# Two windowed attentions on one core: new schedule tables, and layer A's value matmuls two head groups at a time

## The chip, the cores and the metric

The kernel runs on one core of a Trainium2 chip. The metric is the device time of one execution in microseconds (us). Three runs of the kernel before took 1783.95, 1785.1 and 1788.92 us, median 1785.1. One more execution was profiled.

The core's engines run side by side, each through its own instructions in program order: TensorE (PE: matmuls, and weight loads as PEld), VectorE (DVE), ScalarE (ACT), GpSimd (POOL) and SyncE (SP, which here issues copies). They wait for each other on semaphores only.

## The reference

Two attention layers over separate inputs of 2048 rows and 1024 columns, 32 heads of 32, all in float32; their outputs are joined along the last axis.

```python
qkv = (x @ wqkv) ...; q, k, v = qkv[0], qkv[1], qkv[2]; scale = Dh ** -0.5
# layer A: 8 keys per query, every second position back
W, dil = 8, 2
logits = einsum("bhsd,bhswd->bhsw", q, kg) * scale      # kg, vg: gathered keys, values
o_A = softmax(where(mask, logits, -1e9)) @ vg ; out_A = o_A @ wo
# layer B: the 256 keys up to the query
scores = einsum("bhqd,bhkd->bhqk", q, k) * scale
mask = (i - j >= 0) & (i - j < 256)
o_B = softmax(where(mask, scores, -1e9)) @ v ; out_B = o_B @ wo
return concatenate([out_A, out_B], -1)
```

## The kernel before

**Units.** The work is eight units in order: units 0 to 3 are layer B's four stretches of 512 rows ("dense"), units 4 to 7 layer A's ("window"). Layer A's rows are sorted into even and odd ones first, so that a step of two positions becomes a step of one. In each unit the 32 heads are eight groups of four, numbered s = 0 to 7.

**Exact products.** A float32 operand is split into a rounded high part and the rest, and each product is three matmuls (`TERMS`). Splitting a weight or an x tile that was loaded into `raw` takes a cast (L232 on ACT or L235 on DVE) and a subtraction on DVE (L238). Loads into `raw` go out on POOL's queue (L181), three buffers in turn; a buffer's next load goes out when the split of the tile in it is done.

**Work on PE, per unit.** Projections of q and k: per group two blocks of 24 matmuls of 128x128 by 512 (L614). Values: one part of four groups and two of two groups (L683). The output projection of the unit before: eight blocks of 24 (L747). These form one long list, `gemm`, whose order the tables `V_AT`, `O_AT`, `EDGES_V` write out: which slot s holds which value part and output block, and at which item of a unit's last slot the next unit's x tiles ("x0" to "x3") and first weights ("q0", "v0", "v1", "k7") are split.

**Attention of a dense group.** Scores in 16 matmuls (L1024), each into one of four score banks (ring `rs`); row maximum on DVE (L1029), exponential and row sum on ACT (L1034). Then the logarithm of the sums, a small matmul that turns it over (L1063), scores again the other way round (L1108), exponential into `pbuf` (L1115), masks on POOL or DVE (L1093, L1096), and the values in 64x32 tiles of the array (L1173).

**Attention of a window group.** `window(u, s)`: 64 score matmuls in 32x64 tiles (L820) into the four banks of `rs`; mask, softmax on DVE and ACT (L828 to L856) in `band[s % 2]`; two transposes (L859) and sixteen copies on ACT (L868, L871) into `wide[s % 2]`; then `values`, 64 or 72 matmuls in 64x32 tiles (L892) into two banks, the single bank of ring `ro` and one of `rs`; last `overlap` adds the halves where windows overlap and splits the result into an `ot` tile (L981 to L994), an operand of the output projection. `ot` tiles and x tiles share 19 seats (`seats_x`). The scores of group s+2 wait until the values of group s have been issued (`done["o"]`), since they share `band` and `wide`, and until all four score banks are free.

**Who sets the order.** Everything is issued by hand-made order: a planner runs at build time. `Clock` keeps an estimate of when each engine is free; four lists (`aux`, `twos`, `ones`, `gemm`) hold PE's items in order, each with a `ready` time, and the loop at the end always takes the item that could start first. `ones` holds the scores, `twos` the later steps of attention. Only the order comes out of it; on the chip the semaphores decide. The tables shift its estimates: `PACE` per unit (offsets for masks, keys, row data and values, bias of splits, and last the step k of a block at which the next weight is split), `LATE` (added to the time at which a group's q and k are ready for scores), `HOLD` (added to the time at which its values may start), `AHEAD` (added to the step k). `seats_x.used`, `give` and `defer` keep account of what comes free.

Of the kernel before, what the change touches and what calls it, by code (L numbers as in the profile page):

```python
# [36 lines left out]
O_AT = ({2: (0, 1), 3: (2, 3), 4: (4, 5), 5: (6, 7)}, {3: (0, 1), 4: (2, 3), 5: (4, 5), 7: (6, 7)}, {2: (0, 1), 3: (2, 3), 4: (4, 5), 5: (6, 7)}, {2: (0, 1), 3: (2, 3), 4: (4, 5), 6: (6, 7)}, {3: (0, 1), 4: (2, 3), 5: (4, 5), 6: (6, 7)}, {2: (0, 1), 3: (2, 3), 4: (4, 5), 5: (6, 7)}, {1: (0,), 2: (1,), 3: (2, 3), 4: (4,), 5: (5,), 6: (6, 7)}, {1: (0,), 2: (1, 2), 3: (3, 4), 5: (5, 6), 6: (7,)})
EDGE_AT = (0, 1, 2, 3, 4, 5, 6, 7)
EDGES_V = (((2, 'k7'), (5, 'v0'), (14, 'q0'), (15, 'x0'), (18, 'v1'), (27, 'x1'), (29, 'x2'), (33, 'x3')), ((1, 'k7'), (1, 'x0'), (10, 'v0'), (11, 'v1'), (20, 'x1'), (20, 'x2'), (32, 'q0'), (33, 'x3')), ((3, 'k7'), (10, 'v0'), (13, 'v1'), (15, 'x0'), (22, 'x1'), (26, 'x2'), (27, 'q0'), (31, 'x3')), ((5, 'k7'), (6, 'v0'), (12, 'x0'), (14, 'q0'), (17, 'v1'), (18, 'x1'), (24, 'x2'), (32, 'x3')), ((2, 'k7'), (5, 'x0'), (10, 'v0'), (16, 'v1'), (17, 'x1'), (22, 'x2'), (26, 'q0'), (28, 'x3')), ((0, 'k7'), (7, 'v0'), (13, 'x0'), (14, 'v1'), (17, 'q0'), (20, 'x1'), (26, 'x2'), (31, 'x3')), ((2, 'k7'), (10, 'x0'), (10, 'v0'), (15, 'v1'), (16, 'x1'), (26, 'x2'), (29, 'q0'), (33, 'x3')), ((2, 'k7'), (7, 'v0'), (14, 'x0'), (17, 'v1'), (17, 'q0'), (21, 'x1'), (25, 'x2'), (29, 'x3')))
EDGES_K = (((0, 'x0'), (2, 'x1'), (5, 'q0'), (6, 'x2'), (10, 'x3'), (15, 'k0')), ((1, 'q0'), (1, 'x0'), (3, 'x1'), (7, 'x2'), (11, 'x3'), (16, 'k0')), ((0, 'x0'), (4, 'x1'), (4, 'q0'), (8, 'x2'), (12, 'x3'), (16, 'k0')), ((0, 'x0'), (2, 'x1'), (5, 'q0'), (6, 'x2'), (10, 'x3'), (15, 'k0')), ((1, 'q0'), (1, 'x0'), (3, 'x1'), (7, 'x2'), (11, 'x3'), (16, 'k0')), ((0, 'x0'), (2, 'x1'), (5, 'q0'), (6, 'x2'), (10, 'x3'), (15, 'k0')), ((0, 'x0'), (4, 'x1'), (4, 'q0'), (8, 'x2'), (12, 'x3'), (16, 'k0')), ((0, 'x0'), (2, 'x1'), (5, 'q0'), (6, 'x2'), (10, 'x3'), (15, 'k0')))  # L40
LATE = ((7, 0, 1.5, 0, 0, 0, 0, 0), (1.5, 3, 5.5, 2, 0, 0, 0, 0), (0, 1.5, 0, 0, 0.5, 3, 0, 0), (0, 0, 0, 0, 0, 0, 0, 0), (0, 0, 0, 4, 0, 0, 0, 0), (0, 0, 0, 0, 0, 0, 0, 0), (0, 0, 0, 0, 0, 0, 0, 0), (0, 0, 0, 0, 0, 0, 0, 0))
ROWS = ((0, 0, 0, 0, 0, 0, 0, 0), (0, 0, 0, 0, 0, 0, 0, 0), (0, 0, 0, 0, 0, 0, 0, 0), (0, 0, 0.4, 0, 0, 0, 0, 0), (0, 0, 0, 0, 0.2, 0, 0, 0), (0, 0, 0, 0, 0, 0, 0, 0), (0, 0, 0, 0, 0, 0, 0, 0), (0, 0, 0, 0, 0, 0, 0, 0))
HOLD = ((0, 1.2, 0, 0, 0, 0, 0, 0), (0, 0, 0, 0, 0, 0, 0, 0), (0.6, 0, 0, 0, 0, 0, 0, 0), (0, 0, 0, 0, 0, 0, 0, 1.2), (0, 0, 0, 0, 0, 0, 0, 0), (0, 0, 0, 0, 0, 0, 0, 0), (-0.4, 0, 0, 0, 0, 0, 0, 0), (0, 0, 0, 0, 0, 0, 0, 0))
AHEAD = ((0, 0, 0, 2, 0, 0, 0, 0), (0, 0, 0, 0, 0, 0, 0, 0), (1, 0, 0, 3, 0, 0, 0, 0), (0, 0, 0, 0, 3, 0, 3, 0), (0, 0, 0, 0, 0, 2, 0, 0), (0, 0, 0, 0, 0, 0, 0, 0), (2, 0, 0, 0, 0, 0, 0, 0), (0, 0, 0, 0, 0, 0, 0, 0))
EARLY, WARM = 1.0, 10
ONES_AT = 5.0, 34.0
TERMS = ((0, 0), (0, 1), (1, 0))
# [2 lines left out]
class Clock:  # L50
# [6 lines left out]
    HOLD = dict(sp=0.63, act=0.35, pool=0.6)  # L57
# [202 lines left out]
def kernel(ctx, tc, xs, wqk, wv, wo, outs, units):  # L260
# [67 lines left out]
    for p in plan:  # L328
# [19 lines left out]
        else:  # L348
            u = p[1] - 1
# [15 lines left out]
    seats_x = Tiles(xpool, ck)  # L365
# [113 lines left out]
    rg, rs, ro, rx = Ring(psg, 2, "g"), Ring(pss, NS, "s"), Ring(pso, 1, "o"), Ring(psx, 1, "x")  # L479
# [7 lines left out]
    def latest(*ts):  # L487
        return None if any(t is None for t in ts) else max(ts)


    def qk_items(u, s):
# [54 lines left out]
        def evac(t, ps, bank):  # L546
# [7 lines left out]
            def low():  # L554
# [86 lines left out]
    def v_items(u, part):  # L641
# [149 lines left out]
    def window(u, s):  # L791


        has_halo = units[u][3]
        buf = s % 2
        hg = u * NG + s
        vp, vc = vparts[parts_of(u)][s]
        v = vbufs[parts_of(u)][vp]
# [4 lines left out]
        def p16():  # L803
            return band[buf][:, :1536].rearrange("p (i c) -> p i c", c=96)[:, :, 24:]

        h = {}

        def scores_ready():
            return latest(rs.empty(), done["stack"].get((u, s)),
# [64 lines left out]
                h["p"] = t + PACE[u][3] + HOLD[u][s]  # L874

        def values_ready():
            if not seats_x.free:
                return None
            return latest(done["v"].get((u, vp)), h.get("p"), ro.when(), rs.when())

        def values():
            h["o"], _ = ro.take()
            h["o2"], bank = rs.take()
            halves = [h["o"], h["o2"]]
            blocks = [(-1, 1, 0, 8)] if has_halo else []
            blocks += [(b, i, P * b + 64 * i, min(72, S - P * b - 64 * i)) for b in range(4) for i in range(2)]
            seen = set()
            for b, i, q0, w in blocks:
                c = 136 * b + 8 + 64 * i if b >= 0 else 0
                r = slice(64 * i, 64 * i + 64)  # L890
                for j in range(4):
                    nc.tensor.matmul(halves[i][32 * j:32 * j + 32, q0:q0 + w],  # L892
                                     v[r, (4 * u + b) % 6, vc + 32 * j:vc + 32 * j + 32], wide[buf][r, j, c:c + w],
                                     start=(i, j) not in seen, stop=True, skip_group_check=True)
# [440 lines left out]
```

## Time and profile before

| | |
|---|---|
| median of three runs | 1785.1 us |
| profiled execution | 1786.24 us |
| its span, first to last instruction | 1784.5 us |
| granted PE clock, mean | 0.999 |
| DVE, ACT, POOL busy | 71%, 59%, 20% |
| HBM read, written | 164.63 MB, 23.07 MB |

How to read the rows: the page gives busy time per engine; PE's is modelled from pipelined matmuls, so that starts, not durations, tell what a matmul costs in a run of them. In the timeline a row has its start, its length, engine, line, operation, output<-inputs, tile of the array, shape and count of merged instructions; square brackets hold the idle time of the engine before it and what ended that.

### The profile page before, as it was taken

The numbers are of one execution on the slowest core, as the hardware profiler recorded it, in microseconds if no ns is written. First come the engines' busy times: TensorE is split into PE (matmuls) and PEld (weight loads), VectorE is DVE, ScalarE is ACT, GpSimd is POOL, SyncE is SP. The second block draws the span as 40 slices with busy tenths as digits, with TensorE's granted clock in tenths as the row PEclk, the third lists the DMA queues.
The fourth block names the chain that finished last, engine by engine and source line by source line (L and its number), as shares of the span: only waits on it lengthen the run. The fifth ranks groups of instructions, "written<-read, shape, count | busy, mean of one in ns | idle before, by whom it ended". The sixth has DMA issues, their size and how long they took to land.

```text
span 1784.5 us, 39512 instructions
## 1 busy us (share of the span) xinstructions
PE 1770.5 (99%) x15210; PEld 1472.7 (83%) x15210; DVE 1268.0 (71%) x2742; ACT 1054.9 (59%) x2630; POOL 365.3 (20%) x776
## 2 busy tenths in 40 slices
PE   9999999999999999999999999999999999999999
PEld 7788888888888888888888888878888888888887
DVE  5668777777777779766667486876678666857863
ACT  5677666765667666676667355554555354534552
POOL 3222322123222313222233300110001100110000
PEclk9999999999999999999999999999999999999999
DMA  6556654647455456454653344444434443543432
GB/s 207 154 154 166 174 146 145 166 134 213 129 152 165 145 156 179 136 158 119 173 159 122 126 130 131 145 132 129 139 123 136 143 136 114 156 139 128 130 104 83
DMA packets 109724, 257.52 MB, mean 144 GB/s; under 512 B 14560, under 2 KB 29920, under 8 KB 109536
## 3 DMA queue, kind: packets, MB, share of 16 engines
q0 software_dynamic: 41760, 152.06, 27.6%
q1 hardware_dynamic: 58560, 86.15, 18.1%
q10 hardware_dynamic: 9216, 16.78, 2.5%
q8 instruction: 120, 1.97, 0.4%
q14 instruction: 68, 0.56, 0.1%
HBM read 164.63 MB, written 23.07 MB: 105 GB/s over the span
## 4 chain that ended last, share of the span: by engine, by line
PE 90%; DVE 4%; ACT 3%; DMA 2%; issue 1%; POOL 0%; SPq 0%; POOLq 0%; DVEq 0%; ACTq 0%
PE g L614 31%; PE g L747 16%; PE g L683 13%; PE s L1108 6%; PE x L614 6%; PE s L1024 5%; PE o L1173 3%; PE x L747 3%; PE x L683 2%; PE s L820 1%; DVE w L238 1%; PE x L1173 1%; DMA raw<-wv 1%; PE s L892 1%; ACT wide L868 1%
## 5 line engine op out<-in xcount | busy, mean ns | idle before, releaser
L614 PE MATMUL g<-x,w 128*128 128x512 f32 x2568 | 643.1, 393 | 0.8 <-ACT x L232 0.5
L614 PEld LDWEIGHTS g<-x,w 128*128 128x128 f32 x2568 | 476.4, 189 | 90.1 <-ACT x L232 1.0
L238 DVE TENSOR_TENSOR w<-raw,w 128x512 fp32r<-128x512 f32 x514 | 336.1, 695 | 44.6 <-ACT w L232 38.1
L1029 DVE CUSTOM_DVE_ANT_0 s<-s,mask_d 128x384 f32<-128x384 f32 (+2 forms) x512 | 262.1, 554 | 100.7 <-PE s L1024 99.6
L683 PE MATMUL g<-w,x 128*128 128x256 f32 (+1 forms) x1872 | 329.6, 320 | 1.2 <-DVE w L238 0.6
L1034 ACT ACTIVATE s<-s,nm 128x384 f32<-128x384 f32 (+2 forms) x512 | 273.8, 536 | 67.3 <-DVE nm L1029 65.7
L683 PEld LDWEIGHTS g<-w,x 128*128 128x128 f32 x1872 | 276.1, 190 | 25.0 <-DVE w L238 1.7
L747 PE MATMUL g<-ot,w 128*128 128x512 f32 x1200 | 296.2, 393 | 0.0
L747 PEld LDWEIGHTS g<-ot,w 128*128 128x128 f32 x1200 | 221.8, 188 | 43.4
L1093 POOL TENSOR_SCALAR_AFFINE_SELECT pbuf<-pbuf 128x256 f32<-128x256 f32 (+1 forms) x445 | 182.6, 435 | 212.8 <-ACT pbuf L1115 202.3
L1115 ACT ACTIVATE pbuf<-s 128x512 f32<-128x512 f32 (+1 forms) x368 | 188.9, 602 | 56.3 <-PE s L1108 50.8
L235 DVE CAST w<-raw 128x1024 fp32r<-128x1024 f32 x181 | 125.9, 695 | 67.9 <-PE g L614 24.6
L181 POOL DMA_DIRECT2D raw<-wqk x126 | 68.0, 540 | 511.9 <-DVE w L238 317.7
L1024 PE MATMUL s<-kst,qst 96*128 96x384 f32 (+2 forms) x512 | 142.2, 339 | 2.8 <-ACT s L1034 2.6
L868 ACT COPY wide<-wide 32x256 f32<-32x256 f32 x256 | 103.4, 404 | 45.8 <-DVE wide L859 42.2
L1108 PE MATMUL s<-qst,kst 128*128 128x128 f32 (+2 forms) x704 | 126.4, 307 | 0.6 <-ACT pbuf L1115 0.3
L614 PE MATMUL x<-x,w 128*128 128x512 f32 x504 | 121.8, 393 | 0.0
L1108 PEld LDWEIGHTS s<-qst,kst 128*128 128x128 f32 x704 | 107.9, 189 | 16.9 <-ACT s L1034 2.3
L1024 PEld LDWEIGHTS s<-kst,qst 96*128 96x128 f32 x512 | 92.7, 189 | 24.1 <-ACT s L1034 6.6
L614 PEld LDWEIGHTS x<-x,w 128*128 128x128 f32 x504 | 93.3, 188 | 20.2
L1034 ACT ACTIVATION_READ_ACCUMULATOR s<-s,nm 128x1 f32 x512 | 105.5, 206 | 0.2
L181 POOL DMA_DIRECT2D raw<-wv x72 | 46.4, 644 | 257.8 <-DVE w L238 97.1
(111 smaller groups left out, 1930.6 us busy)
## 6 DMA issues: line engine op xcount, KB each, us to landing
raw<-wqk POOLq DMA_DIRECT2D x126, 512.0 KB, 4.0
raw<-wv POOLq DMA_DIRECT2D x72, 512.0 KB, 4.4
raw<-wo POOLq DMA_DIRECT2D x64, 512.0 KB, 3.9
qst<-nat SPq DMA_DIRECT2D x96, 256.0 KB, 4.1
kst<-nat SPq DMA_DIRECT2D x96, 256.0 KB, 5.4
raw<-xs POOLq DMA_DIRECT2D x28, 512.0 KB, 4.9
outs<-ost ACTq DMA_DIRECT2D x56, 256.0 KB, 2.6
kst<-halo SPq DMA_DIRECT2D x72, 128.0 KB, 2.8
```

Of the source, the lines that this page charges most:

```text
L235: nc.vector.tensor_copy(t[:, 0, :], raw)
L238: nc.vector.tensor_tensor(t[:, 1, c:c + 512], raw[:, c:c + 512], t[:, 0, c:c + 512].bitcast(F32), op=ALU.subtract)
L614: nc.tensor.matmul(h["ps"], h["w"][:, a, k * P:(k + 1) * P], xt[u][k][:, b, :], start=(k == 0 and i == 0), stop=(k == NK - 1 and i == 2))
L683: nc.tensor.matmul(ps, xt[u][kw * g + k][:, a, p0:p0 + P], h["w"][g][:, c, k], start=(first and t == 0 and half == 0), stop=(last and t == 2),
L747: nc.tensor.matmul(h["ps"], w[:, a, c:c + P], ot[u, k][:, b, :], start=(k == 0 and i == 0), stop=(k == NK - 1 and i == 2))
L868: nc.scalar.copy(diag[r:r + 32, :, :, c:c + 32], pieces[r:r + 32, :, :, 1 + i % 2, :])
L1024: nc.tensor.matmul(ps[:, :n], q[0:96, j, b * P:(b + 1) * P], kk[0:96, j, c0:c1], start=True, stop=True)
L1029: nc.vector.tensor_tensor_reduce(ps[:, :n], ps[:, :n], mask[:, cut:full], scale=-1.0, scalar=BIG, op0=ALU.add, op1=ALU.min, accum_out=nm)
L1034: nc.scalar.activation(ps[:, :n], ps[:, :n], AF.Exp, bias=nm, scale=-1.0, accum_out=sm)
L1093: nc.gpsimd.affine_select(w, w, pattern=[[0, m], [step, n]], compare_op=ALU.is_ge, fill=0.0, base=base, channel_multiplier=chan)
L1108: nc.tensor.matmul(ps[:, x:x + w], kk[:, j, 256 + kb * P:256 + (kb + 1) * P], q[:, j, q0:q0 + w], start=True, stop=True)
L1115: nc.scalar.activation(w, ps[:, :m * n].rearrange("p (j n) -> p j n", j=m), AF.Exp)
```

## The change

First, the values of a window group can be issued together with its neighbour's. `PAIRS` names the pairs, by unit: groups 0 and 1 and groups 4 and 5 of unit 4, 0 to 3 in two pairs of unit 5, 0 and 1 of unit 6, 0 and 1 and 4 and 5 of unit 7. The even group of a pair adds no item to `twos`; the odd group's item runs both groups' values in a row, and then both `overlap`s. It becomes ready when both groups' softmaxes are done, two seats are free and all four score banks are. The even group's first bank is then one of `rs` instead of `ro`'s.

```diff
+PAIRS = ((), (), (), (), (0, 2), (0, 1), (0,), (0, 2))
...
-        h = {}
+        h = pairs[hg % 2] = {}
...
         def values_ready():
-            if not seats_x.free:
+            if len(seats_x.free) < len(both):
                 return None
-            return latest(done["v"].get((u, vp)), h.get("p"), ro.when(), rs.when())
+            return latest(done["v"].get((u, vp)), *[x.get("p") for x in both], ro.when(),
+                          rs.when() if alone else rs.empty())
 
         def values():
-            h["o"], _ = ro.take()
+            own = ro if alone or s % 2 else rs
+            h["o"], first_bank = own.take()
             h["o2"], bank = rs.take()
...
+            return lambda: overlap(u, s, h, bank, own, first_bank, 0 if has_halo else 1)
+
+        alone = s // 2 not in PAIRS[u]
+        h["values"], both = values, [h] if alone else list(pairs)
+
+        def two():
+            ends = [x["values"]() for x in both]
+
             def after():
-                overlap(u, s, h, bank, 0 if has_halo else 1)
+                for f in ends:
+                    f()
 
             return after
 
-        return [Item(scores_ready, scores, CW)], [Item(values_ready, values, C3 + CP)]
+        return [Item(scores_ready, scores, CW)], [Item(values_ready, two, C3 + len(both) * CP)] if alone or s % 2 else []
...
-            ro.give(0, e)
+            own.give(first_bank, e)
```

Second, entries of the tables. In each line stand unit and place, old and new value:

```text
PACE     unit 1 mask bias for POOL 0.1 -> 0.4; unit 2 last entry 0 -> 2; unit 3 value cost 0.0 -> 0.4, last 2 -> 1;
         unit 4 last 2 -> 3; unit 7 bias of splits 0.5 -> -0.5
O_AT     unit 2: blocks 6, 7 in slot 6, were in 5
         unit 3: {2: (0,), 3: (1, 2, 3), 4: (4, 5), 5: (6,), 7: (7,)}, was {2: (0, 1), 3: (2, 3), 4: (4, 5), 6: (6, 7)}
EDGES_V  unit 1: q0 at 28, was 32;  unit 2: x1 at 19, was 22, x2 at 30, was 26;  unit 3: x2 at 28, was 24
         unit 5: x0, x1, x2, x3 at 11, 18, 24, 29, were 13, 20, 26, 31
         unit 6: x0 at 8, was 10; v0 at 11, was 10
LATE     unit 0 group 3: 0 -> 1.5
         unit 1 groups 4 to 7: 0, 0, 0, 0 -> -0.5, 0.5, 4, 4.5
         unit 2 groups 0, 3, 6, 7: 0, 0, 0, 0 -> 3, 4, -0.5, 4;  unit 3 group 0: 0 -> 2
HOLD     unit 1 group 4: 0 -> 1.2;  unit 2 groups 2, 7: 0, 0 -> 1.6, -0.4;  unit 3 group 0: 0 -> 1.2
AHEAD    unit 1 group 4: 0 -> -2;  unit 2 group 7: 0 -> 1;  unit 3 group 6: 3 -> 4
```

More of the change, by code (lines that the diff above doesn't have):

```diff
@@ L34 @@
 ORDER = (0, 1, 2, 3, 4, 5, 6, 7)
-PACE = ((0.4, 2.4, 0.1, 0.1, 0.4, -99, 4), (0.1, 1.8, 0.3, 0.1, 0.4, -99, 2), (0.1, 0.6, 0.3, 0.1, 0.0, -99, 0), (0.2, 2.4, 0.3, 0.1, 0.0, -99, 2), (6.0, 8.0, 0.5, 0.5, 1, 2), (2.0, 6.0, 1.5, 0.2, 1, 2), (4.0, 7.0, 0.5, 0.2, 1, 3), (4.0, 7.0, 0.5, 0.0, 1, 1))
+PACE = ((0.4, 2.4, 0.1, 0.1, 0.4, -99, 4), (0.4, 1.8, 0.3, 0.1, 0.4, -99, 2), (0.1, 0.6, 0.3, 0.1, 0.0, -99, 2), (0.2, 2.4, 0.3, 0.1, 0.4, -99, 1), (6.0, 8.0, 0.5, 0.5, 1, 3), (2.0, 6.0, 1.5, 0.2, 1, 2), (4.0, 7.0, 0.5, 0.2, 1, 3), (4.0, 7.0, -0.5, 0.0, 1, 1))
@@ L36 @@
 V_AT = ({0: 0, 4: 1, 7: 2}, {0: 0, 3: 1, 7: 2}, {0: 0, 5: 1, 7: 2}, {0: 0, 5: 1, 7: 2}, {0: 0, 4: 1, 7: 2}, {0: 0, 6: 1, 7: 2}, {0: 0, 6: 1, 7: 2}, {0: 0, 6: 1, 7: 2})
[L37 removed]
+O_AT = ({2: (0, 1), 3: (2, 3), 4: (4, 5), 5: (6, 7)}, {3: (0, 1), 4: (2, 3), 5: (4, 5), 7: (6, 7)}, {2: (0, 1), 3: (2, 3), 4: (4, 5), 6: (6, 7)}, {2: (0,), 3: (1, 2, 3), 4: (4, 5), 5: (6,), 7: (7,)}, {3: (0, 1), 4: (2, 3), 5: (4, 5), 6: (6, 7)}, {2: (0, 1), 3: (2, 3), 4: (4, 5), 5: (6, 7)}, {1: (0,), 2: (1,), 3: (2, 3), 4: (4,), 5: (5,), 6: (6, 7)}, {1: (0,), 2: (1, 2), 3: (3, 4), 5: (5, 6), 6: (7,)})
@@ L42 @@
 ROWS = ((0, 0, 0, 0, 0, 0, 0, 0), (0, 0, 0, 0, 0, 0, 0, 0), (0, 0, 0, 0, 0, 0, 0, 0), (0, 0, 0.4, 0, 0, 0, 0, 0), (0, 0, 0, 0, 0.2, 0, 0, 0), (0, 0, 0, 0, 0, 0, 0, 0), (0, 0, 0, 0, 0, 0, 0, 0), (0, 0, 0, 0, 0, 0, 0, 0))
-HOLD = ((0, 1.2, 0, 0, 0, 0, 0, 0), (0, 0, 0, 0, 0, 0, 0, 0), (0.6, 0, 0, 0, 0, 0, 0, 0), (0, 0, 0, 0, 0, 0, 0, 1.2), (0, 0, 0, 0, 0, 0, 0, 0), (0, 0, 0, 0, 0, 0, 0, 0), (-0.4, 0, 0, 0, 0, 0, 0, 0), (0, 0, 0, 0, 0, 0, 0, 0))
-AHEAD = ((0, 0, 0, 2, 0, 0, 0, 0), (0, 0, 0, 0, 0, 0, 0, 0), (1, 0, 0, 3, 0, 0, 0, 0), (0, 0, 0, 0, 3, 0, 3, 0), (0, 0, 0, 0, 0, 2, 0, 0), (0, 0, 0, 0, 0, 0, 0, 0), (2, 0, 0, 0, 0, 0, 0, 0), (0, 0, 0, 0, 0, 0, 0, 0))
+HOLD = ((0, 1.2, 0, 0, 0, 0, 0, 0), (0, 0, 0, 0, 1.2, 0, 0, 0), (0.6, 0, 1.6, 0, 0, 0, 0, -0.4), (1.2, 0, 0, 0, 0, 0, 0, 1.2), (0, 0, 0, 0, 0, 0, 0, 0), (0, 0, 0, 0, 0, 0, 0, 0), (-0.4, 0, 0, 0, 0, 0, 0, 0), (0, 0, 0, 0, 0, 0, 0, 0))
@@ L45 @@
+AHEAD = ((0, 0, 0, 2, 0, 0, 0, 0), (0, 0, 0, 0, -2, 0, 0, 0), (1, 0, 0, 3, 0, 0, 0, 1), (0, 0, 0, 0, 3, 0, 4, 0), (0, 0, 0, 0, 0, 2, 0, 0), (0, 0, 0, 0, 0, 0, 0, 0), (2, 0, 0, 0, 0, 0, 0, 0), (0, 0, 0, 0, 0, 0, 0, 0))
+PAIRS = ((), (), (), (), (0, 2), (0, 1), (0,), (0, 2))
 EARLY, WARM = 1.0, 10
@@ L444 @@
     halo = [[dram.tile([P, 2, 256], F32, name=f"halo{i}_{s}") for s in range(NG)] for i in range(2)]
+    pairs = [None, None]
     xt, xready, ot, rows = {}, {}, {}, {}
@@ L967, in join, with overlap @@
         ck.defer(r, add)
-    def overlap(u, s, h, bank, first):
+    def overlap(u, s, h, bank, own, first_bank, first):
         hg = u * NG + s
```

4 lines of the change are left out of this document (2 added, 2 removed).

## The prediction

> **What bounds the kernel now.** I read the page first, then the busy time by stage, then what TensorE (PE) waited for, and last the instructions in order of time around the waits and around two visits to small tiles.
>
> ```profile
> span 1784.5 us, 39512 instructions
> PE 1770.5 (99%) x15210; PEld 1472.7 (83%) x15210; DVE 1268.0 (71%) x2742; ACT 1054.9 (59%) x2630; POOL 365.3 (20%) x776
> PE 90%; DVE 4%; ACT 3%; DMA 2%; issue 1%; POOL 0%; SPq 0%; POOLq 0%; DVEq 0%; ACTq 0%
> ```
>
> The chain of work that ended last is PE for 90%, so only three things can move the end: PE instructions that go or come, the time PE loses when it changes between whole-array and small-tile matmuls, and the time in which it waits. The next view gives the busy time in six stretches: layer B's unit 0 and the start of unit 1, the rest of unit 1, unit 2, unit 3, then layer A in two halves.
>
> ```profile
> 0.00:326.00 326.00, 321.27 (x2233) 264.80 (x2234) 227.89 (x627) 222.70 (x597) 94.10 (x235) 1.00 0.60 165
> 326.00:488.00 162.00, 159.72 (x1219) 132.96 (x1218) 122.99 (x317) 105.52 (x273) 42.01 (x83) 0.99 0.56 159
> 488.00:742.00 254.00, 253.41 (x2020) 213.16 (x2019) 194.00 (x511) 173.53 (x446) 67.77 (x137) 1.00 0.54 155
> 742.00:1017.00 275.00, 275.00 (x2112) 230.39 (x2112) 181.52 (x465) 179.35 (x452) 86.00 (x188) 1.00 0.49 142
> 1017.00:1383.00 366.00, 364.39 (x3806) 302.32 (x3805) 271.53 (x412) 192.76 (x443) 38.27 (x68) 1.00 0.43 135
> ```
>
> After a width and PE's busy time stand PEld, DVE, ACT and POOL; near the end is the granted clock. Unit 1 is the one that sticks out: 2.28 us of open idling in 162 us and the only clock below 1.00; unit 3 idles not at all. Who made PE wait, in total, times, longest:
>
> ```profile
> PE s L1024 <- ACT s L1034: 2.6, 4, 0.9
> PE x L683 <- DVE w L238: 1.1, 1, 1.1
> PE s L1063 <- DVE hl L1055: 0.7, 2, 0.6
> PE g L683 <- DVE w L238: 0.6, 1, 0.6
> PE g L683 <- ACT vbuf L633: 0.5, 1, 0.5
> ```
>
> So all the waiting there is to win is a handful of single events. A steady run of whole-array matmuls gives the unit of account:
>
> ```profile
> 1498.61 4.24 PE L614 MATMUL g<-x,w 128*128 128x512 f32 x18
> 1502.69 0.52 PE L683 MATMUL x<-w,x 128*128 128x256 f32 x3
> ```
>
> Eighteen starts in 1502.69 - 1498.61 = 4.08 us: 0.227 us each (the 4.24 us includes the last one's pipelined tail).
>
> **The change, part by part. (a) Seven pairs.** A visit of one group of heads to the 64x32 tiles looks like this:
>
> ```profile
> 1042.71 2.20 PE L747 MATMUL g<-ot,w 128*128 128x512 f32 x9
> 1044.85 0.27 PE L892 MATMUL o<-wide,vbuf 64*32 64x72 f32 x4
> ...
> 1045.45 0.27 PE L892 MATMUL s<-wide,vbuf 64*32 64x64 f32 x4
> 1045.65 1.66 PE L747 MATMUL g<-ot,w 128*128 128x512 f32 x6
> 1047.14 1.07 PE L747 MATMUL x<-ot,w 128*128 128x512 f32 x4
> ```
>
> From 1042.71 to 1047.14 are 4.43 us, for 15 whole-array matmuls (15 x 0.227 = 3.40) and one visit: 1.03 us. Inside, 60 of its 64 matmuls start within 0.60 us, so all 64 take 0.64 to 0.66. The rest, 0.37 to 0.39 us, is the price of going in and out: on entry 2.14 us for nine where 2.04 is due (0.10), some 0.14 between the last tile and the next whole matmul, and 0.13 more in the six behind it (1.49 us for 6 x 0.227 = 1.36). A pair keeps both groups' 128 matmuls and drops one such price. At most 0.39 is saved; at least the entry's 0.10, if the loss behind a visit grows with its length. No visit of 128 matmuls is in the trace; I take 0.35, close to the one measured. 7 x 0.35 = **-2.4 us** (bounds -0.7 and -2.7).
>
> What it moves: the even group's values wait for the odd group's softmax, and the pair needs all four score banks free where one was needed. Behind it stand only the scores of the next two groups. In unit 5 group 1's values and group 2's scores are:
>
> ```profile
> 1229.11 0.21 PE L892 MATMUL s<-wide,vbuf 64*32 64x8 f32 x4
> ...
> 1235.61 0.94 PE L820 MATMUL s<-pbuf 32*64 32x72 f32 x64
> ```
>
> Group 2's scores already come 6.5 us after group 1's values, so with groups 0 and 1 together at 1229 they need not move, and projections fill PE meanwhile. I cost the delay at 0; without this cover it would be one late split per pair (a rival below). Each pair's ACT and DVE instructions stay the same in number, back to back; no DMA is added.
>
> **(b) The last part of unit 1.** Here are PE's and DVE's instructions where the next unit begins; then two stretches with the granted clock third from the end (0.89, 0.53); then two pieces of the chain of work:
>
> ```profile
> 437.80 0.51 PE L1024 MATMUL s<-kst,qst 96*128 96x384 f32 x2
> 439.21 0.44 PE L1024 MATMUL s<-kst,qst 96*128 96x384 f32 x1 [0.90 <-ACT s L1034]
> 440.29 0.69 PE L1024 MATMUL s<-kst,qst 96*128 96x384 f32 x1 [0.64 <-ACT s L1034]
> 440.78 5.41 PE L614 MATMUL g<-x,w 128*128 128x512 f32 x17
> ...
> 437.77 0.69 DVE L235 CAST w<-raw 128x1024 fp32r<-128x1024 f32 x1
> 438.49 1.29 DVE L238 TENSOR_TENSOR w<-raw,w 128x512 fp32r<-128x512 f32 x2
> ...
> 441.83 0.56 DVE L1029 CUSTOM_DVE_ANT_0 s<-s,mask_d 128x384 f32<-128x384 f32 x1
> ...
> 437.90:440.98 3.08, 1.54 (x6) 0.97 (x5) 3.01 (x7) 2.24 (x6) 0.72 (x1) 0.89 0.96 250
> 440.98:443.90 2.92, 2.92 (x9) 2.25 (x8) 2.88 (x8) 1.24 (x4) 0.73 (x1) 0.53 0.83 229
> 425.44 0.71 PE g L683 x6
> 426.68 0.18 PE s L1024
> ```
>
> Four score matmuls, 0.18 us each when nothing holds them (the last row), take 2.98 us until the next projection: 2.26 lost. DVE does no score's maximum from 437.77 to 441.83, because the split of unit 2's first weights ("q0") and of two x tiles stands in its queue. Then the clock falls to 0.53, and the 17 projections start over 5.41 - 0.39 = 5.02 us (0.39 is one matmul's tail, from the steady run: 4.24 - 17 x 0.2267) where 16 x 0.227 = 3.63 are due: 1.39 more. Together 3.65 us, over half of it hidden from the list of waits.
>
> The Trainium skill, "TensorE: Matmul & The Clock Gate", section "Why this matters for your kernels", asks only that PE has no idle gap over about 3 us. By that rule this stall would cost no clock, (b) would be worth at most 2.26 and the sum 1.4 us less; the trace has the fall after 1.54 us of idling spread over 3.08, so the measurement decides.
>
> The new tables move q0's split four list items ahead (32 to 28; an item of six half-width matmuls takes 0.71 us, the last row but one), so 2.8 us, its load through POOL's queue with it, and hold back the scores of groups 6 and 7 of unit 1 by up to 4 and 4.5 us in the planner's account. The split's 1.98 us leaves this spot. I take **-3.3** (bounds 0, if another collision takes its place, and -3.65).
>
> **(c) The rest of layer B's tables.** They touch group 3 of unit 0, and units 1 to 3: hold-backs, look-ahead positions, five output blocks one slot away, more masks offered to POOL. No instruction is added; the order of all that follows changes. At stake are the other two score waits (2.6 - 1.5 = 1.1) and the log-sum's 0.7. New small waits will come; I take **-0.5** (bounds -1.8, and +3.65 for one new stall like (b)'s). An output block in another slot is the same 24 matmuls: 0.
>
> **(d) Layer A's edges.** x tiles of units 6 and 7 are split two items earlier or one value block one later. They answer to the two DVE waits of 1.1 and 0.6 and, through unit 4's look-ahead moved from step 2 to 3, to the 0.5. An earlier split needs an earlier load through POOL's queue; PE has no wait for a DMA in the list, so that has cover. In unit 7 the splits lean by 1 us more towards DVE, where no wait for a split is on the list: 0. I take **-0.7** (bounds -2.2 and, mirrored, +2.2).
>
> Sum: -2.4 - 3.3 - 0.5 - 0.7 = -6.9. The profiled execution took 1786.24 us (span 1784.5 and 1.7 around it), so 1779.3 for a like one; it lies 1.1 above the median of 1785.1, and for the median I say **1778.2 us**.
>
> **The rivals.** *Pairs pay, the tables do not.* Unit 1's stall turns up elsewhere and small waits trade places: only (a), 1785.1 - 2.4 = 1782.7. For it: (b) is one accident of two queues, and any new order can make another. Against: unit 3 shows 275 us without one.
>
> *Slower: the new order makes more such stalls.* Place: score matmuls of units 1 to 3 meeting weight splits on DVE; price 3.65 each with the clock. If (b)'s stays and three more come, +11.0 - 2.4 = +8.6: 1793.7. From the first extra one (+1.3) the kernel is slower than before, and past two (+4.9) measurably so. For it: ten groups are held back or let go by new amounts at once. Against: one in four units now.
>
> *The pair chokes the queues.* Two softmaxes side by side hold up a weight split at each pair, at the 1.1 us of the longest wait for a split: 7 x 1.1 - 2.4 = +5.3, with (b) to (d) 1785.9. The Trainium skill, "TensorEngine Tiling (Array Packing)", section "Performance Considerations", warns that tiling does not speed up the emptying of PSUM; no wait of PE for that emptying stands in layer A's part but the 0.5. Against: 71% of DVE's time is busy, not more.
>
> *All comes off.* Everything at its better bound short of the last tenths: -2.7 - 3.65 - 1.8 - 2.2 = -10.4: 1774.7.
>
> **How the numbers follow.** About 0.3%, 5.4 us, is what a measurement of this kernel can tell from no change: faster means below 1779.7. My forecast 0.53, its own range 1775.5 to 1781; 0.45 of it below 1779.7. All comes off 0.13. Pairs alone 0.14. Choked queues 0.05. More stalls 0.15. Faster 0.45 + 0.13 = 0.58, slower 0.15, same the remaining 0.27. The range goes from 1773.5 to 1789, leaving out most of the slower case and a little of the best.
>
> **What would show it.** (a) Seven fewer L892 visits, each pair about 1.66 to 1.7 us where two cost 2 x 1.03; a larger loss behind a pair refutes 0.35. (b) No granted clock near 0.5 after the first 10 us, and no L1024 wait of 0.9. (c), (d) The list of PE's waits under 5 us in all. Wrong would be a half-speed stretch in units 1 to 3, or a PE wait on L238 right behind a pair.

## The result, and the profile after

The kernel with the change takes 1780.88 us at the median of 15 runs (1779.49 to 1783.38), the kernel before 1785.71 us (1783.95 to 1788.92, 15 runs on the same chip): a ratio of 0.9972, with a 95% interval from 0.9965 to 0.9979. That is 4.8 us: faster beyond doubt, but with 0.3% inside the interval. The median stays above 1779.7 us, the line below which the prediction would call the kernel faster. The profiled execution took 1781.06 us.

The page of the changed kernel (span; busy time by engine; the chain that ended last):

```profile
span 1779.3 us, 39469 instructions
PE 1766.2 (99%) x15210; PEld 1474.0 (83%) x15210; DVE 1260.9 (71%) x2690; ACT 1048.8 (59%) x2629; POOL 375.4 (21%) x829
PE 90%; DVE 3%; ACT 2%; DMA 2%; issue 2%; POOL 0%; SPq 0%; DVEq 0%; ACTq 0%; POOLq 0%
q8 instruction: 120, 1.97, 0.5%
```

PE has as many instructions as before and still makes up 90% of the chain; the line on the queue q8 is needed further down. Masks have moved from DVE to POOL (DVE 2742 to 2690 instructions, POOL 776 to 829). The same stretches of work as before, cut where the changed kernel has them (columns as before, granted clock third from the end):

```profile
0.00:324.00 324.00, 320.02 (x2235) 264.48 (x2236) 224.12 (x616) 222.67 (x597) 97.14 (x249) 1.00 0.61 166
324.00:482.00 158.00, 157.97 (x1221) 132.48 (x1220) 111.35 (x283) 105.04 (x271) 49.10 (x116) 1.00 0.59 166
482.00:737.00 255.00, 254.02 (x2026) 214.02 (x2026) 193.25 (x509) 175.22 (x448) 66.32 (x139) 1.00 0.54 155
737.00:1011.00 274.00, 273.82 (x2101) 229.07 (x2101) 185.27 (x455) 180.03 (x456) 86.09 (x190) 1.00 0.50 140
1011.00:1378.00 367.00, 363.29 (x3797) 303.00 (x3796) 269.02 (x407) 191.12 (x440) 39.29 (x68) 1.00 0.44 134
```

The rest of unit 1 (second row) is now 158 us with 0.03 idle, where it was 162 with 2.28 idle; layer A's first half (last row) idles 3.7 us where it idled 1.6. What PE waited for, in total, times, longest:

```profile
PE x L685 <- DVE w L239: 1.6, 1, 1.6
...
PE s L896 <- issue: 1.0, 1, 1.0
PE s L1037 <- issue: 1.0, 1, 1.0
PE s L1037 <- ACT s L1047: 0.9, 1, 0.9
PE s L822 <- issue: 0.8, 2, 0.6
PE g L685 <- DVE w L239: 0.7, 2, 0.4
```

(L685, L239, L896, L1037, L822, L616, L749 and L1047 are L683, L238, L892, L1024, L820, L614, L747 and L1034 of before.) The score waits behind ACT fell from 2.6 us to 0.9, but the list has not grown short, 8.4 us in all where it was 9.6: the three rows that "issue" ends, which means that the profile shows nothing PE waited for, are new (L1037's lies in the start, at 35.4 us).

Where the time came from shows when each unit's first projection starts on PE in the two traces:

| stretch | ends before | ends after | change in its length |
|---|---|---|---|
| start and unit 0 | 185.9 | 183.6 | -2.3 |
| unit 1 | 440.8 | 434.3 | -4.2 |
| unit 2 | 694.7 | 687.4 | -0.8 |
| unit 3 | 945.5 | 939.4 | +1.2 |
| unit 4, two pairs | 1151.4 | 1145.1 | -0.2 |
| unit 5, two pairs | 1346.1 | 1342.9 | +3.1 |
| unit 6, one pair | 1541.0 | 1536.8 | -1.0 |
| unit 7, two pairs | 1780.3 | 1775.1 | -1.0 |

So unit 1 gave 4.2 us, more than the 3.3 that its end was to give, units 4, 6 and 7 together about what their five pairs should (5 x 0.35 = 1.75), and unit 5 took 3 us back. In a second profile of the changed kernel (after_again, below) units 1 to 3 change by the same -4.1, -0.8 and +1.1, but unit 5 by +1.0 alone, so not all of the 3 us belongs to the kernel. (The last row ends with PE's last start.)

A pair in the trace (start, length, count; the second row merges PE's small matmuls):

```profile
1421.78 3.11 PE L749 MATMUL g<-ot,w 128*128 128x512 f32 x13
1424.82 0.82 PE L896 MATMUL s<-wide,vbuf 64*32 64x72 f32 x61
...
1426.27 0.96 PE L749 MATMUL g<-ot,w 128*128 128x512 f32 x3
1427.07 2.23 PE L616 MATMUL x<-x,w 128*128 128x512 f32 x9
```

From 1421.78 to 1427.07 are 5.29 us, for 16 whole matmuls (16 x 0.227 = 3.63) and a pair: 1.66 us, where two single visits cost 2 x 1.03. Reckoned in this way, over twelve whole matmuls around each, the seven pairs in their order cost 1.67, 1.75, 3.21, 1.79, 1.67, 1.85 and 1.91 us; those of units 5 and 7 have 72 matmuls a visit, whose single price was 1.07. The third, unit 5's first pair, looks otherwise:

```profile
1222.04 0.92 PE L896 MATMUL s<-wide,vbuf 64*32 64x8 f32 x76
...
1223.44 0.29 PE L896 MATMUL s<-wide,vbuf 64*32 64x64 f32 x3
1224.77 0.30 PE L896 MATMUL s<-wide,vbuf 64*32 64x64 f32 x4 [1.04 <-issue]
1225.01 3.06 PE L749 MATMUL g<-ot,w 128*128 128x512 f32 x12
```

Four matmuls ahead of its end PE stops for over 1 us, and the releaser is "issue": the profile shows nothing that was missing. And unit 5's first scores, 55 us earlier:

```profile
1166.33 0.34 PE L822 MATMUL s<-pbuf 32*64 32x72 f32 x4
1167.23 0.30 PE L822 MATMUL s<-pbuf 32*64 32x72 f32 x2 [0.56 <-issue]
1167.81 0.88 PE L822 MATMUL s<-pbuf 32*64 32x72 f32 x58 [0.28 <-issue]
1168.62 0.50 PE L685 MATMUL g<-w,x 128*128 128x512 f32 x1
1169.37 4.14 PE L685 MATMUL g<-w,x 128*128 128x512 f32 x10 [0.26 <-DVE w L239]
```

Three stops of 1.10 us in all, and behind them ten matmuls over 4.14 us: half speed, 0.62 granted in 1169 to 1173. SP's own queue ahead of them:

```profile
1155.59 8.58 SPq L536 DMA_DIRECT2D pbuf<-nat  x8
```

These eight copies bring the group's queries and keys into row form; the last leaves 2.2 us before the scores. Their late landing makes the two stops by "issue", though the profile names no releaser: the trace has the last copy landing at 1167.72 us, and PE goes on at 1167.81. In after_again and with_pace4, which stop at the same two places, PE goes on 0.09 us behind that landing too. (The landing of the copy before it, which should end the first stop, is not on record.) A later run moves the group.

### The profile page after: what moved, and what is told of

The parts are those of the page before. It is cut to its first block, busy times and chain, and to the rows that moved or that the text cites. A ratio compares the mean times of both kernels' runs of the same rounds, so it can differ in the third digit from the quotient of the medians.

```text
span 1779.3 us, 39469 instructions
## 1 busy us (share of the span) xinstructions
PE 1766.2 (99%) x15210; PEld 1474.0 (83%) x15210; DVE 1260.9 (71%) x2690; ACT 1048.8 (59%) x2629; POOL 375.4 (21%) x829
## 3 DMA queue, kind: packets, MB, share of 16 engines
q8 instruction: 120, 1.97, 0.5%
## 4 chain that ended last, share of the span: by engine, by line
PE 90%; DVE 3%; ACT 2%; DMA 2%; issue 2%; POOL 0%; SPq 0%; DVEq 0%; ACTq 0%; POOLq 0%
PE g L616 30%; PE g L749 16%; PE g L685 14%; PE x L616 6%; PE s L1121 6%; PE s L1037 5%; PE o L1186 3%; PE x L749 3%; PE x L685 2%; PE s L822 1%; PE x L1186 1%; DVE w L239 1%; PE s L896 1%; DMA raw<-wv 1%; DMA raw<-xs 1%
## 5 line engine op out<-in xcount | busy, mean ns | idle before, releaser
L616 PE MATMUL g<-x,w 128*128 128x512 f32 x2568 | 639.3, 392 | 0.6 <-ACT w L233 0.6
L616 PEld LDWEIGHTS g<-x,w 128*128 128x128 f32 x2568 | 475.4, 188 | 89.6 <-ACT w L233 1.0
L239 DVE TENSOR_TENSOR w<-raw,w 128x512 fp32r<-128x512 f32 x514 | 335.9, 695 | 42.8 <-ACT w L233 36.3
L685 PE MATMUL g<-w,x 128*128 128x256 f32 (+1 forms) x1872 | 331.5, 320 | 0.7 <-DVE w L239 0.7
L1047 ACT ACTIVATE s<-s,nm 128x384 f32<-128x384 f32 (+2 forms) x512 | 274.1, 536 | 65.9 <-DVE nm L1042 64.7
L685 PEld LDWEIGHTS g<-w,x 128*128 128x128 f32 x1872 | 277.5, 191 | 24.5 <-DVE w L239 1.4
L749 PE MATMUL g<-ot,w 128*128 128x512 f32 x1200 | 294.5, 392 | 0.0
L749 PEld LDWEIGHTS g<-ot,w 128*128 128x128 f32 x1200 | 222.4, 188 | 43.4
L1106 POOL TENSOR_SCALAR_AFFINE_SELECT pbuf<-pbuf 128x128 f32<-128x128 f32 (+1 forms) x498 | 191.6, 412 | 202.5 <-ACT pbuf L1128 188.5
L236 DVE CAST w<-raw 128x1024 fp32r<-128x1024 f32 x189 | 137.2, 726 | 77.9 <-PE g L616 27.3
L1037 PE MATMUL s<-kst,qst 96*128 96x384 f32 (+2 forms) x512 | 141.1, 338 | 2.1 <-issue 1.0
L616 PE MATMUL x<-x,w 128*128 128x512 f32 x504 | 122.3, 393 | 0.0
L1037 PEld LDWEIGHTS s<-kst,qst 96*128 96x128 f32 x512 | 92.6, 189 | 22.6 <-ACT s L1047 3.1
L616 PEld LDWEIGHTS x<-x,w 128*128 128x128 f32 x504 | 93.3, 188 | 20.2
L1047 ACT ACTIVATION_READ_ACCUMULATOR s<-s,nm 128x1 f32 x512 | 105.9, 207 | 0.2
L182 POOL DMA_DIRECT2D raw<-wo x64 | 35.8, 559 | 322.8 <-DVE w L239 175.5
```

The lines of the kernel that those rows point to most:

```text
L182: self.nc.gpsimd.dma_start(raw if len(ap.shape) == 2 else raw.rearrange("p (a b) -> p a b", a=2), ap)
L236: nc.vector.tensor_copy(t[:, 0, :], raw)
L239: nc.vector.tensor_tensor(t[:, 1, c:c + 512], raw[:, c:c + 512], t[:, 0, c:c + 512].bitcast(F32), op=ALU.subtract)
L616: nc.tensor.matmul(h["ps"], h["w"][:, a, k * P:(k + 1) * P], xt[u][k][:, b, :], start=(k == 0 and i == 0), stop=(k == NK - 1 and i == 2))
L685: nc.tensor.matmul(ps, xt[u][kw * g + k][:, a, p0:p0 + P], h["w"][g][:, c, k], start=(first and t == 0 and half == 0), stop=(last and t == 2),
L749: nc.tensor.matmul(h["ps"], w[:, a, c:c + P], ot[u, k][:, b, :], start=(k == 0 and i == 0), stop=(k == NK - 1 and i == 2))
```

## The experiments

The theory going in: the end of unit 1 is the tables' gain, by the two entries named in the prediction; the pairs save their price wherever they stand; the rest is small. The rival: the tables work only as a set, and a pair's worth hangs on what queues around it. All runs beside the kernel before on the same chip, ratios to it:

| run | what it has | median, us | ratio, 95% interval |
|---|---|---|---|
| tables_only | all new tables, no pairs | 1782.75 | 0.9980 [0.9972, 0.9988] |
| dense_tables | layer B's new tables, no pairs | 1780.9 | 0.9969 [0.9957, 0.9981] |
| pairs_only | pairs, old tables | 1784.28 | 0.9988 [0.9980, 0.9997] |
| after_again | the changed kernel | 1780.06 | 0.9964 [0.9953, 0.9976] |
| u1_q0 | before, and unit 1's q0 at 28 | 1787.2 | 1.0007 [0.9997, 1.0018] |
| u1_late | before, and unit 1's `LATE` | 1785.81 | 1.0005 [0.9996, 1.0014] |
| u1_both | both of these | 1786.91 | 1.0006 [0.9996, 1.0015] |
| dense_and_pairs | layer B's tables, pairs | 1783.44 | 0.9988 [0.9979, 0.9997] |
| with_pace4 | the same, and unit 4's look-ahead 3 | 1779.96 | 0.9966 [0.9951, 0.9981] |
| shift100 | the change, 100 more PE instructions at the start | 1787.8 | 1.0011 [1.0002, 1.0020] |
| rows_later | the change, unit 5's first scores held 2 us | 1782.56 | 0.9978 [0.9968, 0.9988] |
| rows_later_edge5 | the same, unit 5's old edges | 1782.3 | 0.9976 [0.9966, 0.9985] |

The medians of before were 1786.26 (first four), 1785.52 (u1_q0, u1_late, dense_and_pairs, shift100) and 1786.34 us (the others).

### The parts one at a time

```diff
# tables_only: the changed kernel with
-PAIRS = ((), (), (), (), (0, 2), (0, 1), (0,), (0, 2))
+PAIRS = ((), (), (), (), (), (), (), ())
```

> The changed kernel with no pairs (every group of layer A alone), all new tables. If the pairs are worth their seven entries and exits at 0.35 us each less the one stall of 1.3 us seen inside a pair, this is 1 us slower than the changed kernel and about 4 us faster than before (ratio about 0.998). If the pairs carried most of the gain, it is within 1 us of before.

```diff
# dense_tables: tables_only, and layer A's entries back
-PACE unit 4 last 3; unit 7 bias of splits -0.5; EDGES_V units 5, 6 new
+PACE unit 4 last 2; unit 7 bias of splits  0.5; EDGES_V units 5, 6 old
```

> New entries for units 0 to 3 alone, old ones for layer A, no pairs. If the gain is the stall of 3.65 us at the end of unit 1, this is 3.5 us faster than before and shows no granted clock near 0.5 after the first 10 us. If instead part of the difference of the two profiles (2.0 us by 45 us into the span, before any entry acts) is chance of the start, the gain by 1020 us is 3.5, not 5.8 us.

```diff
# pairs_only: the kernel before, with the change's pairs
+PAIRS = ((), (), (), (), (0, 2), (0, 1), (0,), (0, 2))
```

> The changed kernel with every table as before and the same seven pairs. My theory: about 2.4 us faster than before (ratio 0.9987) if no pair stalls inside, 1 us if one does. Rival, that pairs without the new tables choke DVE's queue: slower than before by up to 5 us, with PE waiting on the weight split right behind pairs.

The changed kernel once more, for its spread:

> The changed kernel once more, for a second profile. A stall inside the first pair of unit 5 of 1.2 to 1.3 us again, if it comes from where the pair lies in PE's code; none or another size, if it was chance. The half-speed stretch at the end of unit 4 and the waits of PE on DVE's split at the ends of units 5 and 6 return if the order of the program makes them.

Pairs alone give -2.0 us, layer B's entries alone -5.4, and both are real. Layer A's entries bring nothing by themselves: 0.9980 with them, 0.9969 without, and the intervals overlap. In the profile of dense_tables units 1 to 3 give 3.8 us and the start 2.0, so 3.8 is what layer B's entries are seen to do, and the rest of the 5.4 may be the start's chance. The sum of the two good parts would be -7.4; the whole change has -6.2 here and -4.8 in the main comparison. These intervals are too wide to tell -6.2 from -7.4, or the whole change from layer B's entries alone (0.9969); where the parts do meet is seen further down.

### Unit 1's stall: one entry, the other, both

```diff
# u1_q0: the kernel before with
-EDGES_V unit 1: (32, 'q0')
+EDGES_V unit 1: (28, 'q0')
```

> The kernel before with one table row changed: the first weights of unit 2 split at item 28 of unit 1's last slot, not 32. If the split's place alone made the stall at the end of unit 1, it and the half-speed stretch behind it are gone: about 3 us faster. If the hold-back of groups 6 and 7 is what does it, PE still loses 2 us or more there.

```diff
# u1_late: the kernel before with
-LATE unit 1: (1.5, 3, 5.5, 2, 0, 0, 0, 0)
+LATE unit 1: (1.5, 3, 5.5, 2, -0.5, 0.5, 4, 4.5)
```

> The kernel before with the new hold-backs of groups 4 to 7 of unit 1 alone. Theory that the hold-back does it: stall and half speed gone, about 3 us faster. Theory that the split's place does it: a stall of 1 us or more stays at the end of unit 1.

Both entries together:

> The kernel before with both edits at unit 1's end: the split at item 28 and the new hold-backs of groups 4 to 7. If these two are the cure, PE's lost time in units 1 and 2 falls from 7.6 us to about 3.5 and the kernel is 3 to 4 us faster. If the rest of the dense tables is needed to place what comes after, a new stall of 1 us or more stands after 440 us and the time is within 1.5 us of before.

None is faster than before. In u1_q0 the stall at the end of unit 1 is indeed gone, and a larger one stands 50 us on. Its stretches (columns as above) and its PE there:

```profile
436.00:444.00 8.00, 8.00 (x94) 7.21 (x94) 7.80 (x22) 6.20 (x18) 0.84 (x2) 1.00 1.04 262
488.60:492.20 3.60, 0.45 (x3) 0.06 (x1) 0.00 (x0) 0.71 (x2) 0.48 (x1) 0.97 1.05 345
492.20:495.00 2.80, 2.80 (x8) 2.51 (x9) 1.66 (x6) 0.76 (x2) 0.00 (x0) 0.50 0.30 120
```

```profile
486.72 2.30 PE L614 MATMUL g<-x,w 128*128 128x512 f32 x9
492.17 1.30 PE L1024 MATMUL s<-kst,qst 96*128 96x384 f32 x3 [3.15 <-DMA kst<-nat]
```

PE and DVE both stand still for some 3 us while all 16 DMA engines are busy (share 1.05): PE came earlier to scores whose keys were still on their way through DMA, and the half clock (0.50) follows again. This profiled execution, 1792.0 us, lay above its kernel's median of 1787.2, but 3.8 us of that were lost before unit 1 began, and u1_both has the same thing at the same place:

```profile
487.52 0.76 PE L1024 MATMUL s<-kst,qst 96*128 96x384 f32 x3 [1.97 <-DMA halo<-nat]
```

In both, unit 1 is 2.6 or 2.7 us shorter than before and unit 2 4.2 or 4.3 longer. u1_late keeps a wait of 1.25 us at 439.0 for ACT's pass over the scores, without the fall of the clock, and still gains nothing. In the changed kernel neither the stall nor a successor is there:

```profile
430.00:436.00 6.00, 6.00 (x47) 5.40 (x54) 3.80 (x12) 5.41 (x15) 3.29 (x8) 1.00 0.55 186
436.00:442.00 6.00, 6.00 (x71) 5.01 (x56) 5.96 (x16) 3.36 (x10) 1.30 (x2) 1.00 0.98 221
```

So the gain belongs to the set: in all nine profiles of kernels with layer B's new tables, units 1 to 3 together are 3.2 to 4.1 us shorter than before. The reading that fits is that unit 1's entries take the split out of the way and unit 2's (its first group is held back by 3) put its scores where their keys are there; which of the other entries does it was not tried.

### Where pairs and tables meet

```diff
# dense_and_pairs: the changed kernel with layer A's entries back
-PACE unit 4 last 3; unit 7 bias of splits -0.5; EDGES_V units 5, 6 new
+PACE unit 4 last 2; unit 7 bias of splits  0.5; EDGES_V units 5, 6 old
```

> New entries for units 0 to 3, old ones for layer A, and the seven pairs. If parts add up, 5.4 + 2.0 = 7.4 us faster than before, 1.2 us faster than the changed kernel: the new layer A entries then cost more than they bring. If they were needed for the pairs, it is slower than the changed kernel by 1 us or more.

It came out at -2.1 us: 3.3 us short of layer B's tables alone and 5.3 of the sum. Its longest waits, and ACT, DVE and PE at the start of unit 5 (start, length):

```profile
PE g L685 <- DVE w L239: 5.0, 3, 3.1
```

```profile
1164.40 1.04 ACT L233 CAST w<-raw 128x1024 fp32r<-128x1024 f32 x1
...
1165.47 1.29 DVE L239 TENSOR_TENSOR w<-raw,w 128x512 fp32r<-128x512 f32 x2 [3.25 <-ACT w L233]
...
1166.81 1.34 DVE L854 TENSOR_REDUCE sm<-band 128x16 f32<-128x1152 f32 x1
...
1169.87 1.84 DVE L861 STREAM_TRANSPOSE wide<-band 128x768 f32<-128x768 f32 x2
1171.63 1.25 DVE L239 TENSOR_TENSOR w<-raw,w 128x512 fp32r<-128x512 f32 x2
```

```profile
1169.45 0.39 PE L685 MATMUL g<-w,x 128*128 128x512 f32 x1
1172.94 1.22 PE L685 MATMUL g<-w,x 128*128 128x512 f32 x2 [3.10 <-DVE w L239]
```

Sixteen copies for unit 4's group 6 stand on ACT from 1159.0 us until the cast of a weight at 1164.40. DVE idles 3.25 us for that cast, splits, then runs group 7's softmax and transposes (1166.81 to 1171.6) before the next split, and PE waits 3.10 us for that one. Neither group is in a pair: they are the two behind the pair of groups 4 and 5, and they come late. Group 6's scores start 5.3 us ahead of unit 5's first projection, where dense_tables has 12.4, pairs_only 13.0 and with_pace4, below, 11.7. So it is not the pair's own softmaxes that choke a queue, as the prediction's rival had it at every pair, but the delay of the groups behind a pair, at one edge. Pairs alone don't make it: pairs_only has the same old look-ahead and no such wait, so layer B's new order has a part in it. One entry takes it away:

```diff
# with_pace4: dense_and_pairs with
-PACE unit 4 last 2
+PACE unit 4 last 3
```

> New dense entries, old layer A entries and the pairs, as before this run, with one more entry new: unit 4's look-ahead step 3 instead of 2. If that entry is what the pairs need, the 3.1 us wait of PE on DVE's split at the start of unit 5 goes, and the time is about 5 us better than that kernel's: 7 us faster than before. If another entry is, the wait stays at 2 us or more.

-6.4 us, as good as the whole change, and the wait at this place is 0.20 us:

```profile
1168.93 2.79 PE L685 MATMUL g<-w,x 128*128 128x512 f32 x11 [0.20 <-DVE w L239]
```

Of layer A's entries this one, the look-ahead at which unit 4's weights are split, is the only one whose worth shows in the time: about 4 us (the two intervals just touch) where the pairs and layer B's tables are both there. tables_only has it without pairs and is not faster than dense_tables.

### Unit 5's two stops

The gap inside the pair carries no releaser. The page's q8 line shows 120 packets of instructions, 1.97 MB in all, 16.4 KB each; PE has 2 x 15210 matmuls and weight loads, which makes 65 bytes each if all of it is PE's code. In the gap's neighbourhood (DMA queues from 1222 to 1224) one such packet is moving:

```profile
q8 instruction: 1, 0.02, 2.8%
```

The theory: some 250 instructions lie in a packet; whole matmuls use them slowly (two per 0.227 us), but this pair has 288, 144 matmuls and their weight loads, and starts them within 1.4 us where nothing holds it (1.43 in unit 5's second pair). If the end of what is loaded falls inside it, PE runs dry until the next packet is in. Then 100 more instructions at the very start move the border out of this pair. Ten warm-up matmuls became 60, 58 of them small:

```diff
# shift100: the changed kernel with
-        for i in range(WARM):
+        for i in range(58):
+            nc.tensor.matmul(ps[:, :64], idle[:, :P], idle[:, :64], start=True, stop=True)
+        for i in range(2):
             nc.tensor.matmul(ps, idle[:, :P], idle, start=True, stop=True)
```

> The changed kernel with 100 more instructions in PE's code ahead of everything (58 small matmuls on zeros and 2 full ones for the 10 full ones that warm the clock), order behind them the same. If the gap inside the first pair of unit 5 is PE waiting for its next 16 KB of code, it goes from there (under 0.1 us), and such a gap may turn up in another visit whose place in the code now starts a piece. If it is a wait for data, it stays at 0.5 to 1.2 us.

The start took far longer than meant: the 58 small matmuls needed 12.6 us, and the first projection starts at 14.92 us where it started at 6.0. The time as a whole (1.0011) therefore says nothing. The rows of its waits around the place where L896 stood:

```profile
PE s L1037 <- ACT s L1047: 2.1, 3, 0.9
PE x L685 <- DVE w L239: 1.8, 1, 1.8
...
PE s L822 <- issue: 0.4, 1, 0.4
```

The gap in the pair is gone. Over all eight profiles with this pair PE idles there for 1.04 us in the changed kernel, 0.30 in after_again, 0.33 in with_pace4, 0.34 and 0.59 in the two kernels below, and not at all in pairs_only, dense_and_pairs and shift100.

The traces say more when PE's instructions are counted in order (matmuls, weight loads and waits on semaphores). These are all the stops by "issue" over 0.2 us in runs of small matmuls, but for those of unit 5's first scores:

| place | kernels | instructions before it | idle, us | packet began, us before PE went on |
|---|---|---|---|---|
| unit 5's first pair | after, after_again, with_pace4, rows_later, rows_later_edge5 | 19904 in each | 1.04, 0.30, 0.33, 0.34, 0.59 | 2.45, 2.37, 2.23, 2.25, 2.38 |
| one group's values at 1560 us | tables_only, with_pace4 | 26816 in each | 0.24, 0.25 | 2.96, 3.00 |
| scores at 1139.7 us | pairs_only | 18113 | 0.91 | 2.41 |

18113 lies seven times 256 before 19904 (but for one instruction), 26816 lies 27 times 256 behind it, and a packet of 16384 bytes holds 256 instructions of 64. So three places with nothing in common but their place in the code stop at steps of one packet. In all fourteen traces PE never passes such a step sooner than 2.2 us after the start of the packet that goes with the step before. Unit 5's first pair holds two steps, 24 and 280 instructions into it, and its gap goes by the packet's start: 0.2 us behind the first step where the gap is 1.04, 0.2 to 0.5 ahead of it where the gap is 0.3 to 0.6, 2.5 ahead in dense_and_pairs, which has none. In shift100 both steps come 100 instructions earlier in this work, so that only one is left inside the pair. The theory stands; what starts a packet early or late was not looked into.

The other stop, of unit 5's first scores, comes of row copies that land late. If it alone is what costs time here, holding those scores 2 us would win it back:

```diff
# rows_later: the changed kernel with
-LATE unit 5: (0, 0, 0, 0, 0, 0, 0, 0)
+LATE unit 5: (2, 0, 0, 0, 0, 0, 0, 0)
```

> The changed kernel with the scores of unit 5's group 0 held back by 2 us more in the planner. If PE's stop of 0.9 to 1.4 us inside those scores is the row copies landing late, it goes, with the half speed behind it where that came: 1 to 3 us faster than the changed kernel. If the waits only move to the weight splits of the same slot, no gain.

```diff
# rows_later_edge5: rows_later with unit 5's old edges
-EDGES_V unit 5: (11, 'x0'), (18, 'x1'), (24, 'x2'), (29, 'x3')
+EDGES_V unit 5: (13, 'x0'), (20, 'x1'), (26, 'x2'), (31, 'x3')
```

> As the run before, and unit 5's x tiles split where the kernel before split them (13, 20, 26, 31). If the earlier split makes the longer wait on DVE at the end of unit 5 (1.6 to 2.1 us against 1.2), 0.5 to 0.9 us faster than the run before; if the pairs make it, no change.

No gain in either: 0.9978 and 0.9976 against 0.9972 and 0.9964 of the change itself. PE in rows_later:

```profile
1163.75 4.70 PE L685 MATMUL g<-w,x 128*128 128x512 f32 x20
1170.74 0.96 PE L685 MATMUL g<-w,x 128*128 128x512 f32 x2 [2.30 <-DVE w L239]
1171.63 1.37 PE L822 MATMUL s<-pbuf 32*64 32x72 f32 x64
```

The 64 scores now run through in one piece, but a value matmul ahead of them waits 2.30 us for its weight's split. At this edge two things are late, the rows and the split, and putting off the first only uncovers the second. No run beat the changed kernel by more than the intervals can tell.

The second run shows something else. A wait for a weight's split, in the values of unit 6 at 1362.4 us of the changed kernel, is 1.51 us in rows_later and 1.05 in rows_later_edge5. It is 1.04 to 1.08 us in all nine profiles with unit 5's old edges (1.07 in the kernel before, at 1365.1) and 1.19 to 1.94 in all five with the new ones: the entries that were to shorten this wait lengthen it.

## Why the prediction was right, and where not

**The sum and its parts.** -6.9 was forecast, -4.8 measured (from -3.7 to -6.3 by the ratio's interval): 1780.88 is inside the range and, just, inside the forecast's own 1775.5 to 1781. But it is not below 1779.7, the line for a change that can be told; the outcome between that line and the slower side had 0.27, "faster" 0.58. By its number it is as near to the rival "Pairs pay, the tables do not" (1782.7), but that isn't what happened: layer B's tables alone pay. In the two profiles (b) and (c) together should give -3.8 from units 1 to 3, and these units gave -4.2 - 0.8 + 1.2 = -3.8. (a) and (d) should give -3.1 in layer A, and layer A's units gave -0.2 + 3.1 - 1.0 - 1.0 = +0.9 (-1.2 in after_again). The start gave 2.3 that no term had (1.2 in after_again). Of the signs named beforehand, the seven visits are gone and no stretch of units 1 to 3 is near half clock; but an L1024 wait of 0.90 us stands, and the list of PE's waits is 8.4 us, not under 5.

**(a) The pairs: right in size.** 1.66 us a pair was forecast and is measured, 1.67 to 1.91 in six of the seven; pairs_only has -2.0 [-0.5, -3.6] where -2.4 was due. What failed is the sentence "I cost the delay at 0": the two groups behind a pair come late at the edge of units 4 and 5, and in dense_and_pairs a split stands behind them for 3.10 us. The rival that was kept for this had another mechanism, two softmaxes side by side, and seven times 1.1 us; shown is once 3.1, taken away by one table entry. And the stop of 1.04 us inside one pair was in no term.

**(b) Unit 1's stall: right in size, wrong in its cause.** The step that failed is "The new tables move q0's split four list items ahead ... The split's 1.98 us leaves this spot", taken as the thing that pays. It does leave, and alone that pays nothing (1.0007), nor does the hold (1.0005), nor both (1.0006): what unit 1 wins, 2.6 us in u1_q0, unit 2 loses with 4.2. The bound of 0, "if another collision takes its place", is what these entries do alone; with the whole set of layer B unit 1 is 4.2 us shorter, past the bound of -3.65. (The "ten groups" of a rival are eleven, with unit 2's group 2.)

**(c)** came out at +0.4 in units 2 and 3 where -0.5 was taken: the log-sum's wait at 482.7 us is gone, but a score wait behind ACT near the start of unit 3 grew from 0.59 us to 0.90, at 694.5 us. Its bounds held.

**(d) The step that was wrong.** Layer A's edges were to give -0.7 by two waits for a split. The wait of 1.07 us grew to 1.58 instead (1.94 in after_again), by the new edges of unit 5, and the one of 0.64 is 0.43. Without pairs the entries give nothing that can be told; with pairs and layer B's tables the look-ahead of unit 4 gives about 4 us. And the loss of unit 5 was in no term: the gap in the pair (1.04), the broken scores and the half clock behind them. That loss is the largest part of what stands between the forecast and the profile, eased by the start; in after_again it is 2 us less.

**The clock.** No stretch behind the end of unit 1 stood near 0.5, as the prediction asked; but one did in unit 5, after 1.10 us of stops spread over 3 us:

```profile
1169.00:1173.00 4.00, 3.75 (x11) 2.87 (x11) 3.93 (x7) 3.78 (x13) 0.55 (x1) 0.62 0.44 125
```

That goes further against the rule of the Trainium skill that the prediction weighed, "TensorE: Matmul & The Clock Gate", section "Why this matters for your kernels", which asks only that PE has no idle gap over about 3 us. Nor is it a threshold on the idle time alone: shift100 waits 1.75 us in one piece, up to 1370.26 us (the row of 1.8 above), and keeps a clock of 1.00 behind it.

**The start.** PE, DVE and POOL have the same order in both kernels for the first 107 us, yet the changed one is 2 us ahead by 82. One cast shows it, in the kernel before and then in the changed one:

```profile
25.57 0.69 DVE L235 CAST w<-raw 128x1024 fp32r<-128x1024 f32 x1 [3.25 <-DMA raw<-wv]
```

```profile
23.36 0.69 DVE L236 CAST w<-raw 128x1024 fp32r<-128x1024 f32 x1 [1.32 <-DMA raw<-wv]
```

The same load landed 2 us earlier. Over thirteen profiles the matmul that turns group 1's log-sums (L1063 of before) starts at 83.52 to 88.20 us in the five kernels with the old order of layer B and at 81.93 to 84.21 in the eight with the new one; the two overlap. Whether the change has a part in it stays open; it may be the loads' own chance. A profile's gain of 5.2 us is to be read with this in mind.

## What to carry to other kernels

A stall where two queues meet is worth its size only if what comes next is ready: taking one cause away brought PE sooner to data still in flight, and nothing was won until the following unit's holds were set too. Price such an edit at nothing unless the next waiter can be named and shown to be early. Merging visits to small tiles saved their fixed price, 0.2 to 0.4 us each in six of seven pairs. But it puts off the work of the groups behind them, so look at each place where a weight split stands in that queue; and it makes longer runs of small matmuls, so count the instructions of a run against what one packet of code holds.

## What the runs showed of the hardware

PE can stop in a run of small matmuls for its own code: up to 1.04 us, at steps of 256 of its instructions, and it passed no step sooner than 2.2 us after the packet of the step before began. In all fourteen traces a half-speed stretch behind a stop lasts 3.41 us (once two of them, 6.82) and begins whole multiples of 3.41 us after the clock's first rise. Fifty-eight matmuls of 128x64 that alternate with their weight loads took 12.58 us at the very start (0.22 us each). The clock was then at half: whole matmuls behind them start 0.43 us apart until it rises at 19.1 us. At full clock a visit to 64x32 tiles starts 64 in 0.65.

```profile
1.52 12.58 PE L1272 MATMUL s<-qst 128*128 128x64 f32 x58 [1.52 <-DVE qst L1269]
13.92 1.20 PE L1274 MATMUL s<-qst 128*128 128x512 f32 x2
```
